# Expert 2's first early product ahead of the main part, its weights split by columns, the first late routing chain placed later

## Chip, cores and metric

The kernel runs on one core of a Trainium2 chip. The metric is the device time of one execution in microseconds (us). Below, "run" is the whole timed execution, and "span" the stretch from the first to the last instruction that the profile shows; all points of time in the trace count from the span's start.

## What is computed

An attention layer feeds a mixture-of-experts layer. Attention: batch 4, 8 heads, 1152 positions, head size 64; queries are averaged in pairs, so 576 query rows a head and 4 x 576 = 2304 tokens of 512 features come out. Each token then goes through its two best of 8 experts (512 -> 1024 -> 512):

```python
q_pool = q.reshape(B, H, S // 2, 2, D).mean(axis=3)
attn = softmax(scale * q_pool @ k.T) @ v           # (B, H, 576, 64)
x = attn_out.transpose(0, 2, 1, 3).reshape(2304, 512)

logits = x @ w_gate
noise_scale = np.log1p(np.exp(x @ w_noise))
noisy_logits = logits + noise_scale * noise
top2 = np.argpartition(-noisy_logits, 2, axis=1)[:, :2]
top2_w = softmax over the two chosen logits
for e in range(8):
    for k in range(2):
        mask = top2[:, k] == e
        h = np.maximum(x[mask] @ w1[e], 0.0)
        out[mask] += top2_w[mask, k, None] * (h @ w2[e])
```

## The kernel before

**Stages.** The attention part runs to about 428 us. The expert part needs, for each token, the router's result: tokens are sorted by scattering their rows (indirect DMAs from POOL, helper line L98) into a DRAM table `xg` with one region of rows for each expert, and an expert's rows are then read back transposed (`xload`, L946) as the tile `xT`. Each expert has room for CAP = 640 rows. Most tokens are routed while the attention still runs. The last ones, the "late" tokens in three groups of three 128-row blocks, are routed after it in two chains of small VectorE operations: the first (tiles `rtc`, `ruc`) takes group 0 and ends in 6 scatters, the second (tiles `rta`, `rua`) takes groups 1 and 2 and ends in 12. Both pass PE once: `ruc` or `rua`, written at L815, goes through matmuls against a triangular matrix (L818) and a matrix of ones (L820) for the running positions, and then L824 to L850 write the rows' metadata into the tiles `xr`, which the scatters wait for. The second chain needs the first one's running count `n` (L827, L836).

**Early part.** Rows that are already in `xg` need not wait. For experts 0 and 1, the first EARLY = 256 rows are multiplied before the late rows have come: `mm1` (L989, eight slices f0 to f7 of 128 hidden columns, 12 matmuls of 256 columns each, since fp32 weights are split in a high and a low fp16 part and three products are added), then ReLU and the same kind of split on ACT (`hh`, L1035) and VectorE (`hl`, L1039), then `mm2` (L1006) on two 128-row blocks, 24 matmuls of 512 columns each. All of this, the late routing chains and the weight splits (`split`: ACT writes the high part at L936, VectorE the low part at L938) are operations of one list scheduler (class `Plan`): each has an engine, a cost and a key (a due time on the planner's clock; `LATE` = 440), and when its dependencies are met the planner puts it into its engine's order by key. On the chip the engines run those orders as written, and wait by semaphore.

**Main part.** `run` is written by hand. Expert e in turn: metadata, `mm1` on the rows that are left (384 late rows for experts 0 and 1, in 12 matmuls of 384 columns a slice; all 640 for the others, in 24 matmuls of 320), then `mm2` of expert e - 1 on its remaining blocks (three for experts 0 and 1, five for the others). The splits of `w1` for expert e + 1 lie in the `mm1` loop of expert e, for e from 1 on, the splits of `w2` in the `mm2` loops.

**PSUM.** `mm1` uses two double-bank tiles, `pss0` and `pss1`. In the early part each half of one holds one slice f, so two slices share a tile; in the main part a slice has a whole tile, in turns.

**Loads.** fp32 weights come in pieces of 512 KB, four for `w1` and four for `w2` of an expert, into four "raw" buffers (`kr`, `qr`, `vr`, `kn`, reused from attention; two more pieces lie in the still empty `hl`). A buffer's next load is put behind the VectorE split that frees it. All these loads and the `xT` reads are issued by one in-order queue, SP.

## Time and profile before

| | us |
|---|---|
| runs shown | 875.05, 877.10, 878.53 |
| median | 877.1 |
| the profiled execution, whole run | 875.3 |
| its span | 873.5 |
| PE busy in the span | 805.9 (92%) |
| early part: end of attention's last matmuls to the main part's first | 428.1 to 486.5 |
| main part's last matmul ends | about 862 |

PE is the busiest engine by far. In the main part it never waits; the places where it does lie between 435 and 487 us, where its early products, the late routing chains and the weight splits share the engines. A row of the trace's order of time reads: start, duration, engine, line, operation, output <- inputs, partitions x elements, how many are merged, and in brackets the idle time of the engine before it with what ended it. Matmuls overlap their neighbours, so the distance between two starts, not the duration, is what one costs. The clock column PEclk is 1.00 at 2.4 GHz and 0.50 at 1.2 GHz.

### The profile page before, as it was taken

The numbers are of one execution on the slowest core, as the hardware profiler recorded it, in microseconds if no ns is written. First come the engines' busy times: TensorE is split into PE (matmuls) and PEld (weight loads), VectorE is DVE, ScalarE is ACT, GpSimd is POOL, SyncE is SP. The second block draws the span as 40 slices with busy tenths as digits, with TensorE's granted clock in tenths as the row PEclk, the third lists the DMA queues.
The fourth block names the chain that finished last, engine by engine and source line by source line (L and its number), as shares of the span: only waits on it lengthen the run. The fifth ranks groups of instructions, "written<-read, shape, count | busy, mean of one in ns | idle before, by whom it ended". The sixth has DMA issues, their size and how long they took to land.

```text
span 873.5 us, 21140 instructions
## 1 busy us (share of the span) xinstructions
PE 805.9 (92%) x8685; PEld 533.3 (61%) x8685; DVE 531.7 (61%) x1253; ACT 444.4 (51%) x662; POOL 394.9 (45%) x377
## 2 busy tenths in 40 slices
PE   4798989999999998898889799999999999999994
PEld 1475766677767776676746455666574655647442
DVE  6988899989998899999795141434133232422300
ACT  5677778877877776675442132333233332322210
POOL 4377887989888984586125202010202112030222
PEclk9799999999999999999999999999999999999998
DMA  8899978789898994658858725374728364280242
GB/s 207 203 201 215 194 204 192 200 209 199 202 189 170 212 204 99 162 189 238 129 206 289 124 94 107 102 207 112 177 76 216 68 170 104 98 204 13 28 57 39
DMA packets 213829, 137.80 MB, mean 158 GB/s; under 512 B 150496, under 2 KB 183776, under 8 KB 213728
## 3 DMA queue, kind: packets, MB, share of 16 engines
q1 hardware_dynamic: 205088, 116.33, 55.2%
q0 software_dynamic: 8640, 20.08, 11.4%
q8 instruction: 69, 1.13, 0.6%
q14 instruction: 32, 0.26, 0.1%
HBM read 62.14 MB, written 35.44 MB: 112 GB/s over the span
## 4 chain that ended last, share of the span: by engine, by line
PE 64%; DVE 22%; issue 5%; ACT 4%; DMA 4%; POOL 1%; SPq 0%; POOLq 0%; DVEq 0%; ACTq 0%
PE pss L989 23%; PE psm L1006 21%; PE psm L393 8%; DVE pl L370 6%; PE psm L305 4%; DVE rd L317 4%; PE pss L357 4%; PE pss L358 3%; DVE vv L289 2%; ACT pf L365 1%; DVE kd L299 1%; ACT rd L313 1%; DVE mx L335 1%; DVE qn L289 1%; DMA qt<-qn 1%
## 5 line engine op out<-in xcount | busy, mean ns | idle before, releaser
L373 POOL TENSOR_TENSOR pl<-pf 128x384 f16<-128x384 f32 x282 | 281.0, 1028 | 85.2 <-ACT pf L365 61.0
L365 ACT ACTIVATE pf<-pss 128x768 f32<-128x768 f32 x216 | 173.5, 812 | 64.8 <-PE pss L358 40.6
L98 POOL DMA_INDIRECT out_dram<-y,mti x40 | 62.1, 1553 | 316.1 <-ACT y L1011 310.2
L393 PEld LDWEIGHTS <-pf 128*128 128x128 bf16 x2880 | 156.6, 98 | 38.9 <-issue 13.3
L393 PE MATMUL psm<-vv,pf 128*128 128x65 f16 (+1 forms) x2880 | 168.0, 195 | 4.5 <-DVE vv L289 1.8
L393 PE MATMUL psm<-vv,pl 128*128 128x65 f16 (+1 forms) x1440 | 158.5, 194 | 9.3 <-DVE pl L370 8.7
L357 PE MATMUL pss<-qt,kt 128*128 128x384 f16 (+1 forms) x576 | 148.2, 287 | 3.1 <-ACT pf L365 2.9
L358 PE MATMUL pss<-qt,kt 66*128 66x384 f16 (+1 forms) x576 | 148.8, 288 | 0.0
L999 DVE SCALAR_TENSOR_TENSOR hl<-pss,hh 128x640 f16<-128x640 f32 (+1 forms) x64 | 48.5, 758 | 158.2 <-ACT hh L998 158.2
L393 PEld LDWEIGHTS <-pl 128*128 128x128 f16 x1440 | 127.4, 100 | 14.1 <-DVE pl L370 11.0
L1006 PE MATMUL psm<-wl,hh 128*128 128x512 f16 x320 | 121.3, 379 | 0.0
L1006 PE MATMUL psm<-wh,hl 128*128 128x512 f16 x320 | 121.3, 379 | 0.0
L1006 PE MATMUL psm<-wh,hh 128*128 128x512 f16 x320 | 121.3, 379 | 0.0
L1006 PEld LDWEIGHTS <-hh 128*128 128x128 f16 x640 | 62.6, 98 | 74.0
L998 ACT ACTIVATE hh<-pss 128x640 f16<-128x640 f32 (+1 forms) x64 | 41.6, 650 | 129.3 <-PE pss L989 129.3
L317 DVE CUSTOM_DVE_ANT_0 rd<-psm,rd 128x512 f32<-128x512 f32 x144 | 97.2, 682 | 11.8 <-ACT rd L313 10.4
L1011 ACT ACTIVATE y<-psm,mg 128x512 f32<-128x512 f32 x40 | 27.5, 687 | 150.6 <-issue 77.3
L313 ACT ACTIVATE rd<-psm 128x512 f32<-128x512 f32 x144 | 85.7, 597 | 20.9 <-PE psm L305 13.9
L370 DVE TENSOR_TENSOR pl<-pf 128x768 f16<-128x768 f32 x75 | 90.9, 1227 | 0.8 <-ACT pf L365 0.8
L989 PE MATMUL pss<-xT,fh 128*128 128x320 f16 (+1 forms) x448 | 84.5, 306 | 4.7 <-DMA xT<-xg 4.7
L305 PE MATMUL psm<-kt,qt 128*128 128x128 f16 (+3 forms) x317 | 75.8, 312 | 11.6 <-DVE mx L317 6.2
L989 PE MATMUL pss<-xT,wh 128*128 128x320 f16 (+1 forms) x448 | 83.4, 303 | 0.0
(205 smaller groups left out, 1115.6 us busy)
## 6 DMA issues: line engine op xcount, KB each, us to landing
xg<-zt SPq DMA_DIRECT2D x40, 260.0 KB, 4.9
kr<-in_k_dram SPq DMA_DIRECT2D x32, 288.0 KB, 3.8
vr<-in_v_dram SPq DMA_DIRECT2D x16, 576.0 KB, 4.7
kr<-in_moe_w_dram SPq DMA_DIRECT2D x16, 512.0 KB, 4.3
qr<-in_moe_w_dram SPq DMA_DIRECT2D x16, 512.0 KB, 4.5
kn<-in_moe_w_dram SPq DMA_DIRECT2D x16, 512.0 KB, 4.5
qr<-in_q_dram SPq DMA_DIRECT2D x31, 256.0 KB, 3.3
vr<-in_moe_w_dram SPq DMA_DIRECT2D x14, 512.0 KB, 3.9
```

The lines of the kernel that those rows point to most:

```text
L98: i = nc.gpsimd.indirect_dma_start(out=out, out_offset=bass.IndirectOffsetOnAxis(ap=idx, axis=0), in_=src, in_offset=None, **kw)
L305: s.nc.tensor.matmul(ps[r, o:o + m.shape[1] * P], s.G.buf["qt", i][:, c, r], m, start=True, stop=True)
L313: s.nc.scalar.activation(s.G.buf["rd", i, c], s.G.buf["D", i, c], AF.Relu)
L317: s.nc.vector.tensor_tensor_reduce(out=rd, in0=s.G.buf["S", i, c], in1=rd, scale=1.0, scalar=-3.0e38, op0=ALU.add, op1=ALU.max, accum_out= ...
L357: mm(ps[:, a, o:o + w], kt[:, hh * NK + kc, :], qf[:, q0:q0 + w], start=True, stop=False)
L358: mm(ps[:, a, o:o + w], kt2[0:66, hh * NK + kc, :], qf2[0:66, q0:q0 + w], start=False, stop=True)
L365: s.nc.scalar.activation(s.parts(u)[0], s.G.buf["ps", u][:, :, 0:SG], AF.Exp, scale=0.125 / (IN_SCALE * IN_SCALE))
L370: s.nc.vector.tensor_sub(pl, pf, ph)
L373: s.nc.gpsimd.tensor_sub(pl[:, a], pf[:, a], ph[:, a])
L393: mm(o[:, 0:x], src[:, t % 2, ci * P:ci * P + P], vv[:, hh * NK + kc, a:a + x], start=st, stop=last and src is pl, skip_group_check=True)
L989: nc.tensor.matmul(ps[:, i, 0:N], w[:, dc, f * P:(f + 1) * P], xT[:, 2 * dc + x, i * N:(i + 1) * N], start=(n == 0), stop=(n == 11))
L1006: s.nc.tensor.matmul(ps, h[:, f, b * P:(b + 1) * P], w[:, f, :], start=(f == 0 and k == 0), stop=(f == 7 and k == 2))
```

## The change

It does five things.

- `NFIRST` = 3: expert 2's `mm1` on its first 256 rows is a third set of eight slices in the early part (not its `mm2`). Its rows are read in the early part too (`A.xe[2]`), so in the main part expert 2 has 384 rows left in `mm1`, and all five blocks in `mm2`.
- Its `w1` is therefore split in the early part (four ACT and four VectorE operations out of the main part's loop of expert 1), into a tile of its own, `w1x`, so that `w1` of expert 0, which the main part still reads, stays where it is.
- `w1` of experts 1 and 2 is loaded and split by columns, 256 hidden columns of all 512 features a piece, instead of 128 features a piece: slices f0 and f1 need piece 0 only, f2 and f3 piece 1, and so on. A row of DRAM in such a piece is 1 KB instead of 4 KB.
- The first late chain gets the key 440 instead of 425, and `pace=0.3`; the second 448 instead of 446.
- The four loads for `w1` of expert 3 are issued right behind the late rows' reads, at the head of `run`.

To make room, the tiles for expert rows (`X`) have fixed homes in space that is free by then (`xTg`, `tok2`, `w1x`), and PE's `hh` and `hl` are allocated once.

```diff
--- before.py
+++ after.py
@@ -35,6 +35,7 @@
 XW = 2 * DM + 16
 EARLY = 256
 NEARLY = 2
+NFIRST = 3
 
 IN_SCALE = 64.0
 MC = 32768.0
@@ -581,9 +582,9 @@
             s.open += 1
             if s.open == 4:
                 s.open = 2
-                s.route(R.steps(1, (1, 2), R.A, 0.3, s.half[0]), LATE + 6, [], 0.2, True, then=rows, pace=0.35, first=("DVE", 0.12))
-
-        s.route(R.steps(1, (0,), R.C, 0.3), 425, late[0], 0.2, True, then=rows)
+                s.route(R.steps(1, (1, 2), R.A, 0.3, s.half[0]), LATE + 8, [], 0.2, True, then=rows, pace=0.35, first=("DVE", 0.12))
+
+        s.route(R.steps(1, (0,), R.C, 0.3), 440, late[0], 0.2, True, then=rows, pace=0.3)
         for x in range(2):
             s.route(R.logits(1, 1 + x, lambda x=x: L(x), 0.3, None), 436 + x, late[1 + x], 0.2, True, then=both)
 
@@ -638,8 +639,10 @@
         s.xg = s.dram.tile([E * FULL, XW], U16, name="xg")
         s.A, s.C = ("a", 9, 14, 6), ("c", 3, 18, 8)
         s.group, s.xr, s.pre = [], {}, {}
+        s.tok2 = s.rp.tile([P, 9, XW], F16, name="xr")
         for g in range(3):
-            s.xr[1, g] = s.rp.tile([P, 3, XW], F16, name=f"xr{g}")
+            s.xr[1, g] = s.tok2[:, 3 * g:3 * g + 3]
+        s.xTg, s.nx = s.rp.tile([P, 6, 8, P], F16, name="xTg"), 0
         s.args = wg, wn, noise
 
     def setup0(s):
@@ -697,7 +700,8 @@
         xr = s.xr[j, g]
         xT = []
         for c in range(3):
-            xT.append(s.rp.tile([P, 8, P], F16, name="xTg", bufs=6))
+            xT.append(s.xTg[:, s.nx % 6])
+            s.nx += 1
             nc.sync.dma_start_transpose(out=xT[c], in_=xr[:, c, 0:2 * DM])
             yield (gap, "SP", 1.35) if c < 2 else (WAIT_TR, "PE", 1.1)
         ps = s.B.bank()[:, 0:48].rearrange("p (c e) -> p c e", c=3)
@@ -883,7 +887,7 @@
         s.tc, s.nc, s.B, s.R = tc, tc.nc, B, R
         s.w1, s.w2, s.out = w1, w2, out
         pool = lambda name, bufs: ctx.enter_context(tc.tile_pool(name=name, bufs=bufs))
-        s.x = pool("mx", 2)
+        s.x = pool("mx", 1)
         s.y = pool("my", 4)
         s.sm = pool("msm", 4)
         s.w = pool("mw", 2)
@@ -902,6 +906,16 @@
         s.pre = {}
         for e in range(NEARLY):
             s.X[e, 0], s.G[e, 0] = R.pre[e]
+        z = s.x.tile([P, 5 * F * 2], F16, name="w1x")
+        s.w1x = tuple(z[:, x * 4 * F:(x + 1) * 4 * F].rearrange("p (d f) -> p d f", d=4) for x in range(2))
+        late = R.xTg.rearrange("p c d r -> p (c d r)")
+        rows = R.tok2.rearrange("p c m -> p (c m)")
+        cut = lambda t, a, n: t[:, a:a + 8 * n].rearrange("p (d r) -> p d r", d=8)
+        L = CAP - EARLY
+        s.home = {(0, EARLY): cut(late, 0, L), (1, EARLY): cut(late, 8 * L, L), (2, EARLY): cut(rows, 0, L),
+                  (2, 0): cut(z, 8 * F, EARLY)}
+        for e in range(3, E):
+            s.home[e, 0] = cut(rows, 8 * L, CAP) if e % 2 else cut(z, 0, CAP)
         s.nl = 4
         for c, name in F0.raws.items():
             s.pre[0, "2", c] = B.flat(name)
@@ -916,7 +930,10 @@
             r = s.H[1][1].rearrange("p a b -> p (a b)").bitcast(F32)[:, (s.nl - 5) * F:(s.nl - 4) * F]
         else:
             r = s.B.flat(s.F0.raws[(s.nl - 7) % 4])
-        if nm == "1":
+        if nm == "1" and e in (1, 2):
+            eng.dma_start(r.rearrange("p (d f) -> p d f", d=4),
+                          s.w1[e, :, c * 2 * P:2 * (c + 1) * P].rearrange("(d p) f -> p d f", p=P))
+        elif nm == "1":
             eng.dma_start(r, s.w1[e, c * P:(c + 1) * P])
         else:
             eng.dma_start(r.rearrange("p (a f) -> p a f", a=2),
@@ -926,24 +943,31 @@
     def split(s, e, nm, c, half=None, load=True):
         nc = s.nc
         if c == 0 and half != 1:
-            if nm == "1" and e % 2 == 0:
+            if (e, nm) == (2, "1"):
+                s.W[e, nm] = s.w1x
+            elif nm == "1" and e % 2 == 0:
                 s.W[e, nm] = s.F0.w
             else:
                 s.W[e, nm] = tuple(s.w.tile([P, 4, F], F16, name=f"w{x}{nm}", bufs=int(nm)) for x in "hl")
         hi, lo = s.W[e, nm]
         r = s.pre[e, nm, c]
+        if nm == "1" and e in (1, 2):
+            r = r.rearrange("p (d f) -> p d f", d=4)
+            hi, lo = (t[:, :, c * 2 * P:2 * (c + 1) * P] for t in (hi, lo))
+        else:
+            hi, lo = hi[:, c], lo[:, c]
         if half != 1:
-            nc.scalar.activation(hi[:, c], r, AF.Copy, scale=WS)
+            nc.scalar.activation(hi, r, AF.Copy, scale=WS)
         if half != 0:
-            nc.vector.scalar_tensor_tensor(lo[:, c], r, WS, hi[:, c], op0=ALU.mult, op1=ALU.subtract)
+            nc.vector.scalar_tensor_tensor(lo, r, WS, hi, op0=ALU.mult, op1=ALU.subtract)
             if load:
                 s.load()
 
     def xload(s, e, a, b):
         nc = s.nc
-        s.X[e, a] = s.x.tile([P, 8, CAP], F16, name="xT")
+        s.X[e, a] = s.home[e, a]
         rows = s.R.xg[e * FULL + a:e * FULL + b]
-        nc.sync.dma_start_transpose(out=s.X[e, a][:, :, 0:b - a], in_=rows[:, 0:2 * DM].bitcast(F16))
+        nc.sync.dma_start_transpose(out=s.X[e, a], in_=rows[:, 0:2 * DM].bitcast(F16))
         n = (b - a) // P
         mt = s.sm.tile([P, NB, 8], F32, name="mt")[:, 0:n]
         nc.sync.dma_start(mt.bitcast(U16), rows[:, 2 * DM:].rearrange("(b p) m -> p b m", p=P))
@@ -975,8 +999,6 @@
         nc = s.nc
         hi, lo = s.W[e, "1"]
         xT = s.X[e, a]
-        if e not in s.H:
-            s.H[e] = tuple(s.h.tile([P, 8, CAP], F16, name=f"h{x}") for x in "hl")
         hh, hl = s.H[e]
         if ps is None:
             ps = s.B.wide()
@@ -1024,8 +1046,8 @@
         nc = s.nc
         A.M = s
         s.W[0, "1"] = s.F0.w
-        for e in range(2):
-            s.H[e] = tuple(s.h.tile([P, 8, CAP], F16, name=f"h{x}") for x in "hl")
+        for e in range(E):
+            s.H[e] = s.H[e % 2] if e > 1 else tuple(s.h.tile([P, 8, CAP], F16, name=f"h{x}") for x in "hl")
         fl, ld, done = {}, {}, {}
         G.pool("half", [t[:, a] for t in s.B.wides for a in range(2)])
         last = None
@@ -1043,25 +1065,27 @@
             fl[e, f] = s.late.pop()
 
         los = []
-        for x in range(12):
+        A.xe[2] = op("SP", 1.4, LATE + 21, lambda: s.xload(2, 0, EARLY), lat=4.0)
+        for x in range(16):
             e, nm, c = s.loads[x]
-            key = LATE + (2, 12, 24)[x // 4] + (2, 2.5, 2.5)[x // 4] * c
+            key = LATE + (2, 12, 24, 36)[x // 4] + (2, 2.5, 2.5, 2.5)[x // 4] * c
             hi = op("ACT", 1.06, key, lambda e=e, nm=nm, c=c: s.split(e, nm, c, 0), deps=[ld[x]] if x in ld else ())
             los.append(op("DVE", 1.14, key, lambda e=e, nm=nm, c=c: s.split(e, nm, c, 1, False), deps=[hi]))
-            for y in (4, 5, 6) if x == 0 else (x + 6,) if x < 4 else (x + 4,) if x > 5 else ():
+            for y in (4, 5, 6) if x == 0 else (x + 6,) if x < 4 else (x + 4,) if 5 < x < 12 else ():
                 last = ld[y] = op("SP", 0.6, key, s.load, deps=los[x:x + 1] if y > 5 else (), lat=5.0, after=last)
             done.setdefault((e, nm), []).append(los[-1])
         done[0, "1"] = [A.f0]
-        for e in range(2):
-            k0 = LATE + 23 * e
+        for e in range(NFIRST):
+            k0 = LATE + (0, 23, 46)[e]
             mm, lows = None, []
-            mt = op("DVE", 0.8, k0 + 16, lambda e=e: s.meta(e, 0, EARLY), deps=[A.xe[e]])
+            if e < NEARLY:
+                mt = op("DVE", 0.8, k0 + 16, lambda e=e: s.meta(e, 0, EARLY), deps=[A.xe[e]])
             for f in range(8):
-                mm = op("PE", 1.28, k0 + 1.3 * f, lambda e=e, f=f: one(e, f), deps=done[e, "1"] + [A.xe[e]],
+                mm = op("PE", 1.28, k0 + 1.3 * f, lambda e=e, f=f: one(e, f), deps=(done[e, "1"][f // 2:f // 2 + 1] if e else done[e, "1"]) + [A.xe[e]],
                         take=[("half", ("m", e, f))], after=mm)
                 hi = op("ACT", 0.3, k0 + 1.3 * f + 1, lambda e=e, f=f: act(e, f), deps=[mm])
                 lows.append(op("DVE", 0.33, k0 + 1.3 * f + 1.5, lambda e=e, f=f: low(e, f), deps=[hi], give=[("m", e, f)]))
-            for b in range(2):
+            for b in range(2 if e < NEARLY else 0):
                 for q in range(4):
                     mm = op("PE", 1.28, k0 + 12 + 5 * b + 1.3 * q, lambda e=e, b=b, q=q: s.mm2(e, b, (2 * q, 2 * q + 1), G.buf["y", e, b]),
                             deps=lows[2 * q:2 * q + 2] + done[e, "2"][q:q + 1] if b == 0 else (), take=[("bank", ("y", e, b))] if q == 0 else (), after=mm)
@@ -1071,16 +1095,20 @@
     def run(s):
         s.nc.gpsimd.tensor_copy(s.B.sp, s.X[0, EARLY][0:1, 7, CAP - EARLY - 1:CAP - EARLY])
         s.put()
+        for _ in range(4):
+            s.load()
         for e in range(E + 1):
             if e < E:
-                s.meta(e, EARLY if e < NEARLY else 0, CAP)
+                if e == 2:
+                    s.meta(e, 0, EARLY)
+                s.meta(e, EARLY if e < NFIRST else 0, CAP)
                 for f in range(8):
-                    s.mm1(e, f, EARLY if e < NEARLY else 0, CAP)
+                    s.mm1(e, f, EARLY if e < NFIRST else 0, CAP)
                     s.flush()
-                    if 1 <= e < E - 1:
+                    if 2 <= e < E - 1:
                         s.split(e + 1, "1", f // 2, f % 2)
                 if 1 <= e < E - 1:
-                    s.xload(e + 1, 0, CAP)
+                    s.xload(e + 1, EARLY if e + 1 < NFIRST else 0, CAP)
             if e:
                 for k, b in enumerate(range(2 if e <= NEARLY else 0, NB)):
                     if 2 <= e < E:
```

**VectorE (DVE), end of the second late chain.** Here `rta` and `rua` are that chain's tiles, `wl` <- `qr` and `wl` <- `kn` the low parts of weight pieces; L799/L803 find the best two, L815/L819 write what PE waits for. Before:

```order
L795 MAX rta<-rta 128x8 x6
L938 SCALAR_TENSOR_TENSOR wl_8488<-qr,wh_8487 128x1024
L799 MAX_INDEX rta<-rta 128x8 x6
L803 TENSOR_TENSOR rta<-rta 128x6
L807 CAST rta<-rta 128x12
L810 TENSOR_TENSOR rua<-ev,rta 128x96
L813 MEMSET rua 128x4
L815 TENSOR_TENSOR rua<-rua 128x48
L938 SCALAR_TENSOR_TENSOR wl_8488<-kn,wh_8487 128x1024
L824 TENSOR_SCALAR rta<-rta 128x6
```

After:

```order
L799 MAX rta<-rta 128x8 x6
L803 MAX_INDEX rta<-rta 128x8 x3
L962 SCALAR_TENSOR_TENSOR wl_8456<-kn,wh_8455 128x4x256
L803 MAX_INDEX rta<-rta 128x8 x3
L807 TENSOR_TENSOR rta<-rta 128x6
L811 CAST rta<-rta 128x12
L814 TENSOR_TENSOR rua<-ev,rta 128x96
L817 MEMSET rua 128x4
L819 TENSOR_TENSOR rua<-rua 128x48
L962 SCALAR_TENSOR_TENSOR wl_8541<-kr,wh_8540 128x1024
L828 TENSOR_SCALAR rta<-rta 128x6
```

The split of `kn` (last piece of expert 1's `w1`) has moved from behind `rua` to ahead of it; it is the only operation that this engine has ahead of `rua` now and had not before.

**PE, where the first late chain passes it.** `psm` <- `tri` is the positions' matmul, `xe` the early rows of expert 0 in `mm1`, `hh` and `hl` its hidden rows in `mm2`. Before, between two slices of `mm1`:

```order
L989 MATMUL pss_63<-xe_7750,fl 128x256
L818 LDWEIGHTS tri
L818 MATMUL psm_65<-ruc,tri 128x32
L820 LDWEIGHTS ones
L820 MATMUL psm_65<-ruc,ones 128x24
```

After, within the first block of `mm2`:

```order
L1028 MATMUL psm_67<-wh_8232,hl 128x512
L822 LDWEIGHTS tri
L822 MATMUL psm_66<-ruc,tri 128x32
L824 LDWEIGHTS ones
L824 MATMUL psm_66<-ruc,ones 128x24
```

The chain's matmuls have moved behind all of expert 0's `mm1`; those of the second chain (`rua`), before the change ahead of expert 1's first slice, now stand behind its third.

**SP, the loads of the early part.** `hl`, `qr`, `kn`, `kr`, `vr` on the left are the raw buffers, `w1x` <- `xg` the read of expert 2's early rows. Before:

```order
L920 DMA hl<-in_moe_w_dram 128x1024 x2
L920 DMA qr<-in_moe_w_dram 128x1024
L920 DMA kn<-in_moe_w_dram 128x1024
L922 DMA kr<-in_moe_w_dram 128x2x512
```

After:

```order
L934 DMA hl<-in_moe_w_dram 128x4x256 x2
L934 DMA qr<-in_moe_w_dram 128x4x256
L934 DMA kn<-in_moe_w_dram 128x4x256
L970 DMA_TRANSPOSE w1x<-xg 128x8x256
L973 DMA mt<-xg 128x2x16
L939 DMA kr<-in_moe_w_dram 128x2x512
```

The read of expert 2's rows has come in between the loads of expert 1's weights; the number of weight loads ahead of the late rows' reads is the same.

## Rows read from the trace of the kernel before

**Rows 1.** The page: span, PE's busy time, last chain by engine.

```profile
span 873.5 us, 21140 instructions
PE 805.9 (92%) x8685; PEld 533.3 (61%) x8685; DVE 531.7 (61%) x1253; ACT 444.4 (51%) x662; POOL 394.9 (45%) x377
...
PE 64%; DVE 22%; issue 5%; ACT 4%; DMA 4%; POOL 1%; SPq 0%; POOLq 0%; DVEq 0%; ACTq 0%
```

**Rows 2.** PE's waits, 420 to 490 us: line, releaser, total, times, longest.

```profile
PE pss L989 <- DMA xT<-xg: 4.7, 1, 4.7
PE psm L818 <- DVE rua L815: 2.5, 1, 2.5
PE psm L818 <- DVE ruc L815: 1.7, 1, 1.7
PE pss L989 <- DVE hl L1039: 1.4, 1, 1.4
```

**Rows 3.** PE in order of time, where the stretches of the sum begin.

```profile
439.08 0.18 PE L818 MATMUL psm<-ruc,tri 128*128 128x32 f16 x1 [1.73 <-DVE ruc L815]
441.67 0.56 PE L989 MATMUL pss<-xe,fh 128*128 128x256 f16 x2 [1.44 <-DVE hl L1039]
447.27 0.38 PE L1006 MATMUL psm<-wh,hh 128*128 128x512 f16 x1
460.28 0.19 PE L818 MATMUL psm<-rua,tri 128*128 128x56 f16 x1 [2.49 <-DVE rua L815]
471.31 0.38 PE L1006 MATMUL psm<-wh,hh 128*128 128x512 f16 x1
486.53 0.80 PE L989 MATMUL pss<-xT,fh 128*128 128x384 f16 x2 [4.70 <-DMA xT<-xg]
```

**Rows 4.** Stretches: length, busy PE, PEld, DVE, ACT, POOL, PEclk, DMA, GB/s.

```profile
441.67:445.30 3.63, 3.63 (x18) 2.63 (x18) 3.56 (x7) 0.38 (x1) 3.02 (x3) 0.53 0.92 280
455.00:460.00 5.00, 2.79 (x13) 1.18 (x12) 4.82 (x37) 1.58 (x3) 0.00 (x0) 1.00 0.06 11
471.31:481.68 10.37, 10.37 (x50) 4.67 (x48) 0.85 (x2) 1.45 (x3) 6.20 (x7) 1.00 0.83 324
486.53:489.37 2.84, 2.84 (x10) 1.28 (x9) 0.84 (x8) 0.00 (x0) 1.97 (x3) 0.50 1.18 242
503.56:519.35 15.79, 15.79 (x99) 9.49 (x97) 8.54 (x19) 7.70 (x12) 0.00 (x0) 1.00 0.24 78
534.89:560.97 26.08, 26.08 (x194) 18.76 (x192) 9.17 (x10) 9.39 (x12) 1.55 (x1) 1.00 0.25 71
```

**Rows 5.** VectorE in order of time: both late chains, a split, idle time.

```profile
433.03 0.42 DVE L1039 SCALAR_TENSOR_TENSOR hl<-pss,hh 128x256 f16<-128x256 f32 x1 [1.80 <-ACT hh L1035]
438.85 0.18 DVE L815 TENSOR_TENSOR ruc<-ruc 128x24 f16<-128x24 f32 x1
460.02 0.21 DVE L815 TENSOR_TENSOR rua<-rua 128x48 f16<-128x48 f32 x1
460.45 1.23 DVE L938 SCALAR_TENSOR_TENSOR wl<-kn,wh 128x1024 f16<-128x1024 f32 x1 [0.22 <-issue]
462.86 0.15 DVE L848 COPY xr<-rta 128x6 f32<-128x6 f32 x1
```

**Rows 6.** ACT in order of time, expert 1's last two early slices.

```profile
471.51 0.38 ACT L1035 ACTIVATE hh<-pss 128x256 f16<-128x256 f32 x1 [1.36 <-PE pss L989]
472.39 0.38 ACT L1035 ACTIVATE hh<-pss 128x256 f16<-128x256 f32 x1 [0.49 <-DVE hl L1039]
```

**Rows 7.** VectorE in order of time, the last of the two.

```profile
472.80 0.42 DVE L1039 SCALAR_TENSOR_TENSOR hl<-pss,hh 128x256 f16<-128x256 f32 x1 [0.45 <-ACT hh L1035]
```

**Rows 8.** Chain that ended last, in order of time, last scatter to main part.

```profile
478.38 3.08 DMA xg<-xr,rta
481.47 5.02 DMA xT<-xg
```

**Rows 9.** Loads, 425 to 700 us: tile, count, KB each, median us to landing.

```profile
kn<-in_moe_w_dram SPq DMA_DIRECT2D x10, 512.0 KB, 4.7
```

## The prediction

> **What bounds the kernel now.** I read the page first: PE is busy for 92% of the span, and the chain that ended last is PE's for 64% [rows 1]. So only what PE does or waits for counts, and the next view is the list of its waits around the change [rows 2]. Four waits make 10.3 us, and from 486.53 on the list has no other. In order of time [rows 3] they are: 1.73 for the first late chain's `ruc`, 1.44 for `hl` (VectorE was at the chain and at splits), 2.49 for the second chain's `rua`, and 4.70 for the late rows. The stretches [rows 4] show a second loss: after the first two waits, with 1.15 us of work between them, 18 matmuls took 3.63 us at a granted clock of 0.53, nearly the lower level; the next 18, up to 447.27, took 1.97 [rows 3]. That is 1.66 lost. After the 4.70 the clock was 0.50 and nine matmuls took 2.84 instead of 1.4: 1.4 lost. After the lone 2.49 the clock stayed at 1.00. Together some 13.4 us are to be had. The late rows themselves are a chain of their own: last scatter at 478.38, landed 3.08 later, read by 486.49 [rows 8].
>
> **Work that moves in PE's order.** An early slice costs 12 x 0.109 = 1.31 us (1.97 / 18), so expert 2's eight slices cost 10.5 in the early part. In the main part its `mm1` falls from 192 matmuls, 26.08, to 96 of 384 columns; the same 96 of expert 1, with the same splits beside them that expert 2 has now, took 15.6 (the stretch of 15.79 holds a neighbour or two more) [rows 4]. So 10.5 go out and 10.5 come in: PE's work is conserved, and the gain is what disappears of the 13.4, less new waits. The early 10.5 lie where PE waited 4.70, and push the main part back by the rest.
>
> **VectorE and the two chains.** The order shows that ahead of `rua` VectorE has exactly what it had, plus one split, 1.13 from its start to the next (the row's duration of 1.23 overlaps it by 0.1 [rows 5]). Before, `rua` was ready at 460.2, with 1.80 idle at 431.2 to 433.0 [rows 5] that a ready split of `qr` and others now fill, since the first chain no longer holds them back; the chains' dependent steps also interleave now, which I count at 0.4, between 0 and 2. So `rua` is ready at 460.2 + 1.1 - 1.8 - 0.4 = 459.1; bounds 457.5 and 461.3 (nothing filled). `ruc` was ready at 439.0; ahead of it now stand 7 more `hl` (0.35 each, the row's 0.42 less the overlap [rows 7]), 4 splits (1.13) and 12 steps of the second chain (an estimate of 0.13 each, from the copies' 0.15 [rows 5]): +8.6, less the 1.8 filled and with small waits for data, 446.6.
>
> **PE's walk through the early part.** It is free at 437.35 (439.08 less 1.73 [rows 3]). The router's matmuls cost 1.15, the last three slices of expert 0, 36 x 0.109 = 3.9 at full clock, so `mm2` begins at 442.4 instead of 447.27. `ruc` is met after 18 of its 48 matmuls (0.216 each, 10.37 / 48), at 446.3: wait 0.3, at most 1.5. `mm2` ends at 453.4, and expert 1's first three slices at 457.3; their weights' splits by columns are what lets them go before the last piece is there. Then PE waits for `rua`: 1.8. Slice f3 ends at 460.5; f4 takes the PSUM half of f1 and so waits for its `hl`, behind which VectorE has a split, some chain steps and another `hl`, 2.7 after `rua`: 461.8, wait 1.3. From there the sum is plain: f4 to f7 5.2, `mm2` 10.4, expert 2's slices 10.5, ending at 487.9. The walk in one line: the end is `rua` + 28.8.
>
> **The hand-over to the main part.** The main part's first slice takes the tile `pss1` that expert 2's f6 and f7 hold, and waits for the `hl` of f7. Before, the same pair of expert 1 had PE's end at 471.31, ACT's first at 471.51, and VectorE's last from 472.80 to 473.22 [rows 6, 7]: ACT and VectorE take turns on the tile, 1.9 us. Before, `mm2` covered it; now there is nothing between. Bounds 0.9 (one slice's share) and 2.5. So the main part begins at 489.8. The row that decides is ACT's: it began f6 only after f7 was done. The Trainium skill, "PSUM — Partial Sum Buffer", section "PSUM bank collisions raise a hardware error", forbids two engines on the same bank and quadrant at once, but lets them use different banks; the two halves are different banks, so by that rule f6 could be emptied under f7 and the main part begin on it 1 us sooner. The row disagrees, and I go by it.
>
> **Late rows.** Before, the second chain's metadata was written up to 463.1 (last copies from 462.86 on [rows 5]) and the rows were there at 486.49. In the new order `rua` is followed by a split (1.13), two `hl` (0.7), and the same small steps (some 1.9): 459.1 + 3.7 = 462.8. So the rows land at about 486.5 again, 3.3 us before PE wants them. The first chain's six scatters start some 8 us later but end before 458, ahead of the twelve. The read of expert 2's rows goes in front of four loads on SP; it waits for nothing that is late, and its issue costs them 2 us or so (an estimate: 40% of the 5.02 from issue to landing that a read of 384 rows takes [rows 8]), for which the cover below has room.
>
> **Loads by columns.** The trace has no load in 1 KB rows. The nearest rows are 512 KB loads at 4.7 us [rows 9]; I take 4.7, and bound it by 3 and by twice that. The last piece of `w1x` can be issued when expert 1's last `w2` piece is split, about 467.6, so it is split by 475.3 and needed by about 481.5 (VectorE has it ahead of expert 2's `hl`, on which f4 waits at 482.6). Six us of cover: twice 4.7 costs nothing. The four loads for expert 3 behind the late reads take buffers free since then, and nothing waits: 0 either way.
>
> **The sum.** The main part starts 3.3 later (489.8 - 486.5), runs its first nine matmuls at full clock (-1.4, since no wait before it is over 2) and has 10.5 less: -8.6. Span 873.5 - 8.6 = 864.9; the profiled run was 1.8 longer than its span, so 866.7 against 875.3, and on the scale of the median, 877.1, **868.5**. With the bounds of `rua` (-1.6, +2.2), of the hand-over (-1.0, +0.6) and of the wait for `ruc` (-0.3, +1.2, which the wait for `rua` takes up), the likeliest case spans 866 to 871.
>
> **Rivals.**
> - *The clock falls again.* The waits of 1.8 and 1.3 around f3 are like the pair of 1.73 and 1.44 that ended at 0.53; then the next 18 matmuls cost 1.7 more: 870.2, or 872 with a later `rua`. Against: between them lies a full slice, and the 2.49 alone left 1.00. The Trainium skill, "TensorE: Matmul & The Clock Gate", section "What's actually happening", has the gate follow how busy PE was recently; by that rule two gaps close together weigh more than one alone. The trace agrees: 0.53 after the pair, 1.00 after the single one [rows 4]. Chance 0.18.
> - *The late rows are last again.* If the second chain's metadata come y later than 462.8, the main part starts y - 3.3 later. Twice a split and two `hl` in the way is 3.7; with the scatters delayed by the first chain's six, up to 7: 869 to 873, and the 4.70 wait returns in a smaller form. Chance 0.12.
> - *The halves are handed over singly*, by the bank rule: 867.5. Against it stands ACT's row. Chance 0.05.
> - *The gain is eaten.* Waits for `ruc`, `rua` and `hl` each near their upper bound and both half-clock stretches back (1.7 + 1.4), `rua` at 464 or so: 873 to 880, no change that can be told. Chance 0.08.
> - *Slower.* The column loads: the last `w1x` piece holds up VectorE's in-order `hl`, and so PE, at f4 of expert 2. From 481.5 on each us costs one; to be slower by 4.4 it must come 13 us after that, so the load must take 4.7 + 6 + 13, five times the row. 882 and more. Nothing in the profile points there, the DMA share in 455 to 460 is 0.06 [rows 4]. Chance 0.05.
>
> That the change doesn't do what it says is excluded by the order: expert 2's slices stand ahead of the main part.
>
> **How the numbers follow.** The forecast has 0.52, the rivals 0.18, 0.12, 0.05, 0.08 and 0.05. 0.5% is 4.4 us, about what a measurement here can tell from no change: faster means under 872.7, slower over 881.5. Faster: 0.52 + 0.18 + 0.05 and half of the late rows' case, 0.81; same 0.14; slower 0.05. The range goes from 865.5 (all lower bounds) to 874 (late rows and part of the eaten gain).
>
> **What would show it.** In the profile after: the wait for late rows (4.70) is gone, and PE has two waits of 1 to 2 us between 457 and 462, on L822 and on `hl`; `rua`'s L819 ends at 458 to 460; expert 2's early slices run from about 477 without a wait; PE then waits some 1.9 for `hl`, and the main part begins at 488 to 491 with the clock at 1.00; `mm1` of expert 2 there takes 15.6. I am wrong if `rua` comes after 462, if the main part's first matmul waits for the late rows, or if one of the new weights holds PE.

## The result

The changed kernel takes 867.29 us (median of four runs, 865.85 to 868.18) against 876.08 for the kernel before in the same series: ratio 0.9897, 95% interval 0.9865 to 0.9928, 8.8 us less. The forecast was 868.5. The profiled execution has a span of 866.3 against 873.5 [rows 1], 7.2 less; the two differ also in the attention part, in which all five engines have the same instructions in the same order as before and which ended 2.3 us later in this profile (VectorE's last write of attention's result starts at 430.94, before at 428.61). Points of the two traces are therefore compared below by their distance from that write.

The page after: span, PE's busy time, the chain that ended last by engine and by line.

```profile
span 866.3 us, 21179 instructions
PE 807.5 (93%) x8685; PEld 534.2 (62%) x8685; DVE 533.5 (62%) x1269; ACT 446.1 (51%) x670; POOL 398.5 (46%) x377
...
PE 64%; DVE 22%; issue 4%; ACT 4%; DMA 4%; SPq 2%; POOL 1%; ACTq 0%; DVEq 0%; POOLq 0%
PE pss L1011 23%; PE psm L1028 22%; PE psm L394 7%; DVE pl L371 6%; DVE rd L318 4%; PE pss L358 4%; PE pss L359 4%; PE psm L306 3%; DVE vv L290 2%; DMA kr<-in_k_dram 1%; DVE kd L300 1%; ACT pf L366 1%; DVE qn L290 1%; ACT rd L314 1%; DVE mx L336 1%
```

PE is busy as long as before, in a shorter span, and has the same share of the chain. What became of its waits is in the list for 430 to 500 us (line, releaser, total, times, longest), the answer to [rows 2]:

```profile
PE pss L1011 <- DVE hl L1061: 2.8, 2, 1.9
PE psm L822 <- DVE rua L819: 1.3, 1, 1.3
```

The wait for the late rows (4.7), the wait for `ruc` (1.7) and the one behind it are gone; from 430 to the end of the span 4.1 us are left where there were 10.3. In order of time, as in [rows 3]:

```profile
448.55 0.18 PE L822 MATMUL psm<-ruc,tri 128*128 128x32 f16 x1
460.55 0.19 PE L822 MATMUL psm<-rua,tri 128*128 128x56 f16 x1 [1.34 <-DVE rua L819]
463.15 0.38 PE L1011 MATMUL pss<-xe,wh 128*128 128x256 f16 x2 [0.95 <-DVE hl L1061]
491.25 0.48 PE L1011 MATMUL pss<-xTg,fh 128*128 128x384 f16 x2 [1.87 <-DVE hl L1061]
```

`ruc` is passed at 448.55 with no wait at all, `rua` costs 1.34, f4 of expert 1 waits 0.95 for `hl`, and the main part's first matmul 1.87, for `hl` as well. The stretches (length, busy time of PE, PEld, DVE, ACT, POOL, then PEclk, DMA share, GB/s; compare [rows 4]):

```profile
430.94:436.94 6.00, 6.00 (x42) 4.67 (x41) 3.64 (x14) 4.04 (x6) 0.00 (x0) 0.72 1.26 171
455.00:460.00 5.00, 4.21 (x38) 3.52 (x37) 4.83 (x28) 1.69 (x5) 4.07 (x4) 1.00 0.61 201
460.00:465.00 5.00, 3.50 (x36) 3.00 (x36) 4.98 (x25) 1.75 (x4) 0.83 (x1) 1.00 0.93 314
491.25:494.17 2.92, 2.92 (x18) 1.75 (x18) 1.20 (x9) 0.49 (x1) 1.48 (x1) 1.00 1.18 208
539.55:555.15 15.60, 15.60 (x96) 9.15 (x95) 8.14 (x12) 8.57 (x13) 1.21 (x1) 1.00 0.42 118
```

The third and second row hold the waits for `rua` and `hl`: the clock stayed at 1.00. So it did in the fourth, the first 18 matmuls of the main part, which take 2.92 where nine had taken 2.84. The last row is `mm1` of expert 2 in the main part: 96 matmuls, 15.60 instead of 192 in 26.08. From the main part's first matmul to the end of the span it is 375.05 us now (866.3 - 491.25) and was 386.97 (873.5 - 486.53): 11.9 less. The main part begins 60.31 after attention's last write, before 57.92: 2.4 later. 11.9 - 2.4 = 9.5, less the 2.3 of attention, is the 7.2 of the spans.

Who set the main part's start is in the chain that ended last, in order of time:

```profile
478.91 10.49 PE pss L1011 x96
489.48 0.39 ACT hh L1057
489.90 0.44 DVE hl L1061
490.36 0.39 ACT hh L1057
490.78 0.44 DVE hl L1061
491.25 8.77 PE pss L1011 x53
```

Expert 2's 96 early matmuls take 10.49, with no wait, and then ACT and VectorE take turns on the last tile, from 489.48 to 491.22. On POOL the late rows' first scatter, the last one, and the small copy that follows the landing of the rows show the other candidate:

```profile
464.17 1.41 POOL L99 DMA_INDIRECT xg<-xr,rta  x1 [4.18 <-DVE xr L854]
480.62 0.97 POOL L99 DMA_INDIRECT xg<-xr,rta  x1 [0.31 <-issue]
488.49 0.18 POOL L1096 CAST sp<-xTg 1x1 f32<-1x1 f16 x1 [6.90 <-DMA xTg<-xg]
```

The rows are there at 488.5, 0.9 before PE is through with expert 2 and 2.8 before it starts.

### The profile page after: what moved, and what is told of

The parts are those of the page before. It is cut to its first block, busy times and chain, and to the rows that moved or that the text cites. A ratio compares the mean times of both kernels' runs of the same rounds, so it can differ in the third digit from the quotient of the medians.

```text
span 866.3 us, 21179 instructions
## 1 busy us (share of the span) xinstructions
PE 807.5 (93%) x8685; PEld 534.2 (62%) x8685; DVE 533.5 (62%) x1269; ACT 446.1 (51%) x670; POOL 398.5 (46%) x377
## 4 chain that ended last, share of the span: by engine, by line
PE 64%; DVE 22%; issue 4%; ACT 4%; DMA 4%; SPq 2%; POOL 1%; ACTq 0%; DVEq 0%; POOLq 0%
PE pss L1011 23%; PE psm L1028 22%; PE psm L394 7%; DVE pl L371 6%; DVE rd L318 4%; PE pss L358 4%; PE pss L359 4%; PE psm L306 3%; DVE vv L290 2%; DMA kr<-in_k_dram 1%; DVE kd L300 1%; ACT pf L366 1%; DVE qn L290 1%; ACT rd L314 1%; DVE mx L336 1%
## 5 line engine op out<-in xcount | busy, mean ns | idle before, releaser
L358 PE MATMUL pss<-qt,kt 128*128 128x384 f16 (+1 forms) x576 | 151.4, 293 | 1.0 <-ACT pf L366 0.8
L359 PE MATMUL pss<-qt,kt 66*128 66x384 f16 (+1 forms) x576 | 151.8, 293 | 0.0
L1021 DVE SCALAR_TENSOR_TENSOR hl<-pss,hh 128x640 f16<-128x640 f32 (+1 forms) x64 | 46.4, 724 | 162.1 <-ACT hh L1020 162.1
L394 PEld LDWEIGHTS <-pl 128*128 128x128 f16 x1440 | 127.3, 99 | 15.1 <-DVE pl L371 10.7
L358 PEld LDWEIGHTS <-kt 128*128 128x128 f16 x576 | 57.5, 100 | 21.4 <-issue 8.3
L359 PEld LDWEIGHTS <-kt 66*128 66x128 f16 x576 | 57.4, 100 | 19.0 <-issue 4.2
```

Of the source, the lines that this page charges most:

```text
L358: mm(ps[:, a, o:o + w], kt[:, hh * NK + kc, :], qf[:, q0:q0 + w], start=True, stop=False)
L359: mm(ps[:, a, o:o + w], kt2[0:66, hh * NK + kc, :], qf2[0:66, q0:q0 + w], start=False, stop=True)
L394: mm(o[:, 0:x], src[:, t % 2, ci * P:ci * P + P], vv[:, hh * NK + kc, a:a + x], start=st, stop=last and src is pl, skip_group_check=True)
```

## The experiments

The theory: the early slices fill PE's wait for the late rows, and the moved first chain lets PE get there without waits and at the upper clock; what is left is VectorE's order around `rua` and the hand-over of a PSUM tile. The rivals give the gain to one part alone, or put the late rows last. Each run is compared by ratio with the kernel before, run beside it on the same chip. The first four share one series (before: 876.81).

**Expert 2's early slices at the head of its turn in the main part** (the rest of the change stays):

```diff
-        for e in range(NFIRST):
+        for e in range(NEARLY):
             k0 = LATE + (0, 23, 46)[e]
...
                 for f in range(8):
+                    if e == 2:
+                        s.mm1(e, f, 0, EARLY)
+                        s.flush()
                     s.mm1(e, f, EARLY if e < NFIRST else 0, CAP)
```

> All of the change, but expert 2's first 256 rows are multiplied at the head of its turn in the main part instead of ahead of it. Theory (the early slices fill the gap in which PE waited for the late rows, and the moved chain alone only makes PE reach that gap sooner): PE ends expert 1's early mm2 some 9 us before the late rows are there, waits 9 to 10 us, starts at the lower clock level (1.4 us lost), and mm1 of expert 2 costs 26 us again: 876 us, the time of the kernel before, ratio 0.995 to 1.003. Rival (the chain's new place carries the gain, some 4.8 us of waits and lower clock between 437 and 445): 871 us, ratio 0.994.

Measured: 877.14, ratio 1.0003 (0.9989 to 1.0017). PE's first matmul of the main part, and the stretch that follows it:

```profile
489.77 0.80 PE L1011 MATMUL pss<-xTg,fh 128*128 128x384 f16 x2 [10.54 <-DMA xTg<-xg]
489.77:492.60 2.83, 2.83 (x10) 1.28 (x9) 0.78 (x8) 0.00 (x0) 1.97 (x3) 0.50 1.12 230
```

The wait has grown from 4.70 to 10.54, since PE got there sooner and the late rows did not (58.5 after attention's last write, before 57.9), and the nine matmuls behind it run at 0.50 again, 2.83. The moved chain and the columns alone are worth nothing: what they save in front of the late rows PE waits out. The rival is out. This run also tells what attention's later end is: from attention's last write this profile takes 445.7 us to its end and that of before 444.9, and the medians differ by 0.3. So attention is not longer by 2.3 as a rule with the changed code (the interval leaves some 1.2 either way); the 2.3 belong to the one execution.

**The chains at their old keys:**

```diff
-                s.route(R.steps(1, (1, 2), R.A, 0.3, s.half[0]), LATE + 8, [], 0.2, True, then=rows, pace=0.35, first=("DVE", 0.12))
+                s.route(R.steps(1, (1, 2), R.A, 0.3, s.half[0]), LATE + 6, [], 0.2, True, then=rows, pace=0.35, first=("DVE", 0.12))
...
-        s.route(R.steps(1, (0,), R.C, 0.3), 440, late[0], 0.2, True, then=rows, pace=0.3)
+        s.route(R.steps(1, (0,), R.C, 0.3), 425, late[0], 0.2, True, then=rows)
```

> The change with the two late chains at their old keys (425 and LATE + 6, no pace). Theory: the waits of 1.7 for ruc and 1.4 for hl and the stretch at the lower clock behind them come back (4.8 us), of which the waits for rua and hl around the fourth slice of expert 1 take up only a part, so the main part begins some 4 us later: 871 us, ratio 0.994. Rival (only the early slices count, since the late rows set the main part's start): 867 us, ratio 0.990.

Measured: 872.67, ratio 0.9948 (0.9932 to 0.9965), 4 to 5 us over the change, as expected of the theory. PE's waits in order of time, and the stretch behind the first two:

```profile
441.55 0.18 PE L822 MATMUL psm<-ruc,tri 128*128 128x32 f16 x1 [1.73 <-DVE ruc L819]
444.15 0.38 PE L1011 MATMUL pss<-xe,fh 128*128 128x256 f16 x2 [1.45 <-DVE hl L1061]
467.68 0.38 PE L1011 MATMUL pss<-xe,wh 128*128 128x256 f16 x2 [1.54 <-DVE hl L1061]
495.79 0.49 PE L1011 MATMUL pss<-xTg,fh 128*128 128x384 f16 x2 [1.87 <-DVE hl L1061]
```

```profile
444.15:447.80 3.65, 3.65 (x19) 2.66 (x19) 3.62 (x8) 0.38 (x1) 1.14 (x1) 0.54 0.84 233
```

The pair of 1.73 and 1.45 and the clock of 0.54 are back as in [rows 3, 4], and the wait for `hl` at f4 is 1.54 instead of 0.95. The main part begins 64.7 after attention's last write, 4.4 later than with the change. So with the early slices in the gap each us ahead of it counts, and only then: slices alone 4.1 (876.81 - 872.67), chain alone 0, both 8.8.

**Weights by rows instead of columns:**

```diff
-        if nm == "1" and e in (1, 2):
-            eng.dma_start(r.rearrange("p (d f) -> p d f", d=4),
-                          s.w1[e, :, c * 2 * P:2 * (c + 1) * P].rearrange("(d p) f -> p d f", p=P))
-        elif nm == "1":
+        if nm == "1":
...
-                mm = op("PE", 1.28, k0 + 1.3 * f, lambda e=e, f=f: one(e, f), deps=(done[e, "1"][f // 2:f // 2 + 1] if e else done[e, "1"]) + [A.xe[e]],
+                mm = op("PE", 1.28, k0 + 1.3 * f, lambda e=e, f=f: one(e, f), deps=done[e, "1"] + [A.xe[e]],
```

> The change with w1 of experts 1 and 2 loaded and split by 128 features (4 KB rows in DRAM) instead of by 256 columns. Theory: the first slice of expert 1 now needs all four pieces, the last of which VectorE splits just ahead of rua, so PE waits some 4 us at that slice, perhaps then runs at the lower clock, and the main part begins 2 to 4 us later than with columns: 869 to 871 us, ratio 0.992 to 0.995; the loads land about 1 us sooner, which gives nothing. Rival (columns cost in the loads what they give in the order): 867 us or below.

Measured: 870.51, ratio 0.9914 (0.9889 to 0.9939). PE's waits, and the clock just behind them:

```profile
458.64 0.28 PE L1004 MATMUL pss<-xe,wl 128*128 128x256 f16 x1 [2.42 <-DVE wl L955]
459.98 0.21 PE L822 MATMUL psm<-rua,tri 128*128 128x56 f16 x1 [1.06 <-DVE rua L819]
494.66 0.48 PE L1004 MATMUL pss<-xTg,fh 128*128 128x384 f16 x2 [1.87 <-DVE hl L1054]
```

```profile
460.00:462.00 2.00, 2.00 (x16) 1.50 (x16) 1.64 (x6) 0.93 (x1) 0.00 (x0) 0.50 0.97 283
```

PE waits 2.42 for the low part `wl` in its first slice and 1.06 for `rua`, and then the clock is 0.50; the main part begins 63.4 after attention's last write, 3.1 later than with the change, and 4.0 later counted from `ruc` (46.91 against 42.93, see the next run on why). The theory said 4 us of wait and found 2.4 with a clock drop; the total of 870.51 is in the expected range, the ratio just under it (0.992). The interval of this run meets that of the change, so the trace shows the loss, and the times alone do not. The price of the columns would be in the loads. From 435 to 445 us, where the last two pieces of expert 1's `w1` go into these buffers (tile, count, KB each, median us to landing), with columns and then with rows:

```profile
qr<-in_moe_w_dram SPq DMA_DIRECT2D x1, 512.0 KB, 5.8
kn<-in_moe_w_dram SPq DMA_DIRECT2D x1, 512.0 KB, 6.8
```

```profile
qr<-in_moe_w_dram SPq DMA_DIRECT2D x1, 512.0 KB, 5.6
kn<-in_moe_w_dram SPq DMA_DIRECT2D x1, 512.0 KB, 8.0
```

The first two pieces (`hl`) took 4.4 by columns and 4.5 by rows, the first two of expert 2's `w1` (`kr`, `vr`) 5.2 and 5.2 against 5.9 and 4.2. In sum the loads by rows were not sooner, as had been expected by about 1 us, so no price of the columns shows.

**The other PSUM tile first:**

```diff
         for _ in range(4):
             s.load()
+        s.B.nw += 1
         for e in range(E + 1):
```

> The change with the two PSUM tiles of the main part in the other turn: its first slice takes pss0, which expert 2's f4 and f5 held, instead of pss1 with f6 and f7. Theory (the 1.87 us wait ahead of the main part is the hand-over of one tile from VectorE): the wait is gone, the main part begins 1.9 us sooner, the late rows being there 1.0 us before that: 865.4 us, ratio 0.988. Rival (the late rows are then last): a wait for xT of up to 1 us takes its place, 866 to 867 us.

Measured: 865.80, ratio 0.9877 (0.9856 to 0.9898). PE's first matmul of the main part, and POOL's copy that marks the late rows:

```profile
487.89 0.49 PE L1011 MATMUL pss<-xTg,fh 128*128 128x384 f16 x2
```

```profile
486.84 0.18 POOL L1096 CAST sp<-xTg 1x1 f32<-1x1 f16 x1 [7.01 <-DMA xTg<-xg]
```

The wait is gone, and none for the late rows has come in its place: they were there 1.05 before. The main part began 56.7 after attention's last write, 3.6 sooner than with the change, twice the 1.87. The rest is clock, and lies at the head of the early part. The first 6 us after attention's last write here:

```profile
431.21:437.21 6.00, 6.00 (x85) 5.47 (x84) 5.31 (x18) 4.98 (x8) 0.00 (x0) 1.00 1.27 172
```

1.00 where the profile of the change has 0.72, and that of before 0.76 over its own first 6 us:

```profile
428.61:434.61 6.00, 6.00 (x44) 4.81 (x43) 3.71 (x20) 4.05 (x6) 0.00 (x0) 0.76 1.22 185
```

The program up to there is the same, so this differs from execution to execution. `ruc` shows it: it starts 15.7 after attention's last write here, 17.4 in the change. From `ruc` to the main part, which leaves that out, the change takes 42.93 (491.25 - 448.32) and this kernel 40.95: 1.98 less, as expected.

The runs that follow fell on chips on which attention ended 9 to 20 us later, in the kernel before as well (889.86 and 892.50), so that their times spread more. The stretch from `ruc` to the main part's first matmul and the rest behind it do not spread; the latter is 375.0 to 375.1 us in every one.

**VectorE's order around `rua`, with and without the other tile first:**

```diff
-                s.route(R.steps(1, (1, 2), R.A, 0.3, s.half[0]), LATE + 8, [], 0.2, True, then=rows, pace=0.35, first=("DVE", 0.12))
+                s.route(R.steps(1, (1, 2), R.A, 0.3, s.half[0]), LATE + 8, [], 1.2, True, then=rows, pace=0.35, first=("DVE", 0.12))
...
-            key = LATE + (2, 12, 24, 36)[x // 4] + (2, 2.5, 2.5, 2.5)[x // 4] * c
+            key = LATE + (2, 12, 24, 36)[x // 4] + (2, 2.5, 2.5, 2.5)[x // 4] * c + (4 if x in (7, 8, 9) else 0)
```

The kernel "both" also has the line of the run "tile".

> Two edits on the change: the main part's PSUM turn as in the run tile, and the last piece of expert 1's w1 and the first two of its w2 get keys later by 4 (the second chain's PE steps a later due time, slack 1.2 instead of 0.2), which puts that last w1 split behind rua, and hl of f0 and f1 ahead of the chain's rest. Theory (what is left of PE's loss lies in VectorE's order around rua and in the hand-over): the waits of 1.3 for rua and 0.95 for hl go down to 0.3 together, so expert 2's slices end 2.0 us sooner; the late rows come about 1 us sooner too and then set the start, together 3.0 to 3.6 us sooner than the change: 863.7 to 864.3 us, ratio 0.985 to 0.986. Rival (the late rows or a piece of expert 1's w2 come later and take it back): 865.5 us, ratio 0.988, as with the turn alone.

> The order of the splits as in the run both, the PSUM turn as in the change. Theory: 2.0 us sooner than the change, with the hand-over of 1.9 still there: 865.3 us, ratio 0.988. Rival (VectorE's order is worth nothing since something else holds PE): 867.3, ratio 0.990.

Measured: both 876.66, ratio 0.9868 (0.9816 to 0.9921); the order alone 878.60, ratio 0.9883 (0.9846 to 0.9920). PE's waits in "both" from 456 to 500 us, and its first matmul of the main part:

```profile
PE pss L1011 <- DMA xTg<-xg: 0.8, 1, 0.8
PE pss L1011 <- DVE hl L1061: 0.6, 1, 0.6
PE pss L1011 <- ACT hh L1057: 0.3, 1, 0.3
```

```profile
496.39 0.50 PE L1011 MATMUL pss<-xTg,fh 128*128 128x384 f16 x2 [0.78 <-DMA xTg<-xg]
```

The wait for `rua` is gone and that for `hl` down to 0.56; but the late rows are now last, by 0.78. From `ruc` to the main part it takes 40.58, 2.35 less than the change, not 3.6; the order alone takes 41.36, 1.57 less, not 2.0. What the order gives beyond the tile is 0.4, because the late rows stand there. They had been expected 1 us sooner and were not: `rua` starts 10.7 after `ruc`, in the change 12.0, but the rows are there 40.6 after `ruc`, in the change 40.2. The first of the twelve scatters starts 4.6 after `rua` instead of 3.9, and the twelve take 18.4 from first to last (471.04 to 489.41) instead of 17.4 (464.17 to 481.59). When "both" was run again (below, "both2"), PE's first matmul of the main part and POOL's copy were

```profile
509.14 0.50 PE L1011 MATMUL pss<-xTg,fh 128*128 128x384 f16 x2 [0.95 <-DVE hl L1061]
509.15 0.18 POOL L1096 CAST sp<-xTg 1x1 f32<-1x1 f16 x1 [6.92 <-DMA xTg<-xg]
```

The view names `hl`, which ended at the same moment. But in "tile" PE began on this PSUM tile at 487.89, before ACT had begun on f6 and f7, so it does not need their `hl`, and the copy says that the rows came just then: they were last here too.

**The four loads for expert 3 one by one in expert 1's turn:**

```diff
-        for _ in range(4):
-            s.load()
...
                     s.flush()
+                    if e == 1 and f % 2:
+                        s.load()
```

> The change with the four loads for expert 3's w1 issued one by one within expert 1's turn, as before the change, instead of behind the late rows' reads. Theory (their buffers are free and their splits come a whole turn later): no difference, ratio 0.989 to 0.991. Rival (behind the late rows' reads they take bandwidth from the scatters into the output): up to 1 us faster than the change.

> The change once more, on the same chip as the other three, to compare them with: ratio 0.9885 to 0.991. Its attention part is expected to end at another time than in the first profile (427.7 to 431 us), its main part to begin 58 to 61 us after that.

Measured: 880.09, ratio 0.9888 (0.9843 to 0.9933); the change once more beside it 879.33, 0.9889 (0.9845 to 0.9933). No difference; the intervals alone could not exclude the rival's 1 us, but from the main part's first matmul to the end it is 375.08 us against 375.05. Attention ended at 448.5 in the profile of "again", far outside the 427.7 to 431 expected; the main part began 59.4 later, within the 58 to 61.

**The two better ones and the change, side by side:**

> The run tile again, in one call with the two below. From the spans between attention's last write and the main part's first matmul (56.7 us in tile, 58.8 to 60.3 in the change, by how long PE stays at the lower clock at the head of the early part) and the 375.05 us behind that: 1.9 us below the change, ratio to it 0.9978.

> The run both again. Its main part waited 0.8 us for the late rows, so of the 3.6 us expected of it some 2.5 are left: 2.5 us below the change, 0.4 to 0.6 below tile2. If the two edits add up in full, 3.5 below the change; if the turn alone counts, as tile2.

> The change once more, to compare the two with: ratio to the kernel before 0.9885 to 0.991. From the main part's first matmul to the end again 375.0 to 375.1 us.

Measured: 0.9877 (0.9827 to 0.9928), 0.9845 (0.9794 to 0.9896) and 0.9868 (0.9819 to 0.9916). The times do not tell the three apart: the median with the other tile, 883.24, is even 0.6 above the change's 882.61, where 1.9 below had been expected, and the change's ratio is a little under the expected 0.9885 to 0.991. The stretch from `ruc` to the main part does, in two or three profiles each:

| kernel | first profile, us | later profiles, us |
|---|---|---|
| the change | 42.93 | 42.93 ("again"), 42.93 ("again2") |
| other tile first | 40.95 | 40.90 |
| order and tile ("both") | 40.58 | 40.46 |

So the other tile is worth 2.0 us and both 2.4, in the trace; in the measured times it is not shown that either is faster than the change, since their intervals overlap.

## Why the prediction was right

It was right in the total (868.5 forecast, 867.29 measured) and in the sign, by the mechanism named. By its steps:

- *PE's work moves and is conserved*: 10.49 for expert 2's early slices (forecast 10.5), 15.60 for the rest (15.6).
- *Behind the main part's first matmul*: 1.4 for the clock and 10.5 for `mm1`, 11.9 together; measured 386.97 - 375.05 = 11.92.
- *The main part's start*: forecast 3.3 later, measured 2.4 later.
- *PE's walk*: the wait for `ruc` 0.3, measured 0; for `rua` 1.8, measured 1.34; for `hl` 1.3, measured 0.95; the hand-over 1.9, measured 1.87. The run "tile" shows that the last is the tile's and not the late rows'. The rival by which the halves are handed over singly did not come: ACT began on f6 at 489.48, behind PE's last matmul of f7 (489.40).
- *The clock*: forecast at 1.00 around f3 and at the main part's start; it was. The rival with the lower clock did not come up in the change, but "rowwise" shows how near it was (waits of 2.42 and 1.06, then 0.50).
- *The late rows*: forecast 3.3 before the start, measured 2.8. "both" shows them last as soon as 2.4 are taken off the rest.

The step that failed, though the sum hid most of it, is VectorE's. The prediction had `rua` 1.1 sooner: one more split (+1.1), the 1.80 us of idle time filled (-1.8) and 0.4 for steps that interleave. Measured from attention's last write `rua` starts at 29.35 instead of 31.41, 2.06 sooner. Two of the three terms were wrong, and it is luck that they went opposite ways. VectorE in order of time after the change (rows between are left out):

```profile
435.32 0.42 DVE L1061 SCALAR_TENSOR_TENSOR hl<-pss,hh 128x256 f16<-128x256 f32 x1 [1.78 <-ACT hh L1057]
445.64 0.17 DVE L787 SCALAR_TENSOR_TENSOR rtc<-rtc 128x24 f32<-128x24 f32 x1
445.73 0.18 DVE L752 TENSOR_SCALAR rta<-rta 128x48 f32<-128x48 f32 x1
445.85 0.18 DVE L789 SCALAR_TENSOR_TENSOR rtc<-rtc 128x24 f32<-128x24 f32 x1
448.32 0.17 DVE L819 TENSOR_TENSOR ruc<-ruc 128x24 f16<-128x24 f32 x1
460.29 0.21 DVE L819 TENSOR_TENSOR rua<-rua 128x48 f16<-128x48 f32 x1
```

The idle time is still there, 1.78 on the same `hl`, which stands in the order ahead of everything that could fill it. It goes with PE's clock, since this `hl` waits for a slice of PE's by way of ACT: counted from attention's last write it starts at 4.4 us in the profiles with a clock of 0.72 to 0.76 over the first 6 us, at 3.5 to 3.8 with 0.87 to 0.92, and at 2.7 with 1.00, where the view shows no idle time ahead of it ("tile", "loads", "both"). The last rows of the first chain and of the second alternate, 0.09 to 0.12 apart. The kernel before, at the same kind of step, with the first chain alone:

```profile
434.07 0.18 DVE L764 SCALAR_TENSOR_TENSOR rtc<-rtc 128x24 f32<-128x24 f32 x1
434.29 0.18 DVE L767 TENSOR_SCALAR rtc<-rtc 128x24 f32<-128x24 f32 x1
```

0.22 apart. A step that needs the one just before it starts 0.22 after it; with another chain's step between, one starts each 0.11. What this comes to is a sum over VectorE's rows from attention's last write to `rua`; counted is each operation's distance to the next start, and idle time over 0.15 apart (us):

| VectorE ahead of `rua` | before | "keys" | the change |
|---|---|---|---|
| the 98 steps of both chains (`rtc`, `rta`) | 15.94 | 15.77 | 12.06 |
| splits | 8.01 (7) | 7.92 (7) | 9.08 (8) |
| `hl` and the rest | 5.32 | 5.33 | 5.73 |
| idle | 2.14 | 2.42 | 2.48 |
| start of `rua` | 31.41 | 31.44 | 29.35 |

The same 98 steps take 3.9 us less. In the change 46 of them are followed by an operation that is not of their chain, before and in "keys" 15; and "keys", which is the change with the chains where they were, takes 15.8 for them again. So the saving is that of the chains' new place, and interleaving is the one difference seen between the steps. The term "0.4, between 0 and 2", for which the prediction had no row, was mis-sized by 3.5, and the 1.8 for idle time was worth nothing.

## What to carry to other kernels

A wait for data that come at a fixed time is filled by work that was to be done anyway, and only then does time saved ahead of it count: here the moved chain was worth nothing without the early slices (ratio 1.0003) and 4 to 5 us with them. When work fills a wait to the brim, look at what it leaves behind in the buffers: here the last early slices held the PSUM tile that the main part took first, and starting on the other tile gave the 1.9 us back in the trace. A chain of small dependent steps can be made cheaper by putting a second chain between its steps: here 98 steps took 12.1 us of VectorE instead of 15.9.

## What the runs showed of the hardware

- *Clock.* Two waits of PE close together, 1.73 and 1.45, ended at 0.54, nearly the 1.2 GHz level, with 1.15 us of small work between them; 2.42 and 1.06 ended at 0.50; 1.34 and 0.95, with a full slice of 1.31 between, stayed at 1.00, 2.4 GHz. One of 1.87 alone stayed at 1.00 too; one of 4.70 or 10.54 did not. The level at the head of the early part (from 0.72 to 1.00 over 6 us, up to 1.7 us of time) differed between executions of the same code.
- *Scatters.* One 128-row scatter of the late chains on POOL took 0.96 to 1.99 us over all runs, and one and the same differs between runs: the fourth of the first chain took 0.97 before and 1.69 with the change. Where POOL has other work behind them, as in the attention part, this can move PE: in the profile of the change, attention ran level with that of before until a scatter at 378 us took 1.76 instead of 0.97; the POOL operation behind the scatters started at 384.56 instead of 383.28, PE was 1.27 later from 388.8 on, and attention ended 2.3 later. What made the second half of the 2.3 is not shown.
- *VectorE.* Operations of 24 columns that need the one just before them started 0.22 us apart, and 0.09 to 0.12 apart when another chain's operation stood between (rows above).
